# Block-sparse attention on gathered keys: tiles of two query blocks with the twelve key blocks that they see

## The chip, the cores and the metric

The kernel runs on one core of one Trainium2 chip. The metric is the device time of one execution in microseconds. Three executions of the kernel before took 979.37, 981.89 and 981.99 us, so its time is the median, 981.89 us. The profile is of one more execution, whose span is 978.8 us.

The engines have short names here: PE multiplies matrices (PEld is its weight load), DVE, ACT and POOL work on vectors, and SP issues most transfers to the DMA engines. PE writes its products to PSUM, whose banks hold 512 fp32 numbers per partition.

## The reference

```python
# q, k, v: (4 batches, 8 heads, 768 tokens, 64); blocks of 32 tokens, 24 of them
mask = np.abs(blk_i - blk_j) <= 1
mask = mask | (blk_i == 0) | (blk_j == 0) | (blk_i == 23) | (blk_j == 23)
for qb in range(24):
    for kb in sampled_blocks[qb]:            # three, drawn at random
        mask[qb*32:(qb+1)*32, kb*32:(kb+1)*32] = True
scores = np.where(mask, q @ k.T / 8, -1e9)
attn = softmax(scores)                       # denominator + 1e-9
x = (attn @ v)                               # to (3072 tokens, 512)
h = x @ w_in                                 # 512 -> 2048, weights in float64
out = np.maximum(0.01 * h, h) @ w_out        # 2048 -> 512
```

So a query block in the middle sees its own and the two neighbouring blocks, the first and the last block, and three sampled ones; the first and the last query block see all 24. A sampled block may be one that is seen anyway, or be drawn twice; it counts once.

## The kernel before

All products run on fp16 pairs: an fp32 number is scaled by a power of two and split into a high and a low part. A feed-forward product takes three products of parts, scores take two products whose 128 rows stack high and low parts, and the product with V takes two.

**Attention is dense.** The work is cut into 12 items (batch b, run j of 256 tokens) of 16 units; a unit is 128 queries of one head against all 768 keys. Per unit: PE writes scores of 128x768 to PSUM (`unit_scores`, four products, L541, one buffer of two banks); DVE scales them, adds the mask and takes the row's extreme (L551, `unit_ttr`); ACT takes the exponential and its sum (L556); DVE works out the reciprocal (L561, L562); ACT writes the high part of the weights (L571) and DVE the low part (L577), except for the first 32 units, for which ACT scales (L567) and POOL writes both parts (L568, L575). One transposing transfer on SP turns the pair into `pt`, twelve blocks of 128x128 (L582). Two units share the product with V: twelve products of 256 columns (L592). ACT and DVE evacuate it (L604, L607), and split it into x (L615, L617).

**Masks** for all 768 keys are built once as `masks`, of bf16, by POOL (L241). V and K are prepared per batch: scaled, split and, for K, transposed by SP (L484, `kt`); V stays in SBUF in fp16 parts. Q is prepared per half of a run and transposed twice (L511, L514).

**Feed-forward** runs in chunks of 128 hidden units, 16 an item: 12 products of 256 columns (L631), ACT and DVE take the leaky maximum (L639, L645), ACT writes the high part (L652) and POOL the low part (L655), and 6 products of 512 columns (L664) add to two output banks, which are scaled (L681, L684) and sent out (L687).

**Weights** arrive as the bits of float64. Per 128x512 ACT squares the upper word (L274), DVE shifts and joins (L279, L282, L284) and zeroes tiny values (L287). PE sums the squares for the scale (L201), and ACT and POOL or DVE split.

**The order.** The program is unrolled; every engine runs its instructions in program order. One step per unit issues a piece of each kind of work by a string of letters ("tdocqmxgsvbaph" here: reduction, reciprocal, output product, and so on) and spreads preparations over the steps; from unit 32 on PE is held to the written order. Feed-forward chunks of an item come from 7 steps after its last unit. Weight preparation gets 3.2 pieces a step.

Of the kernel before, what the change touches and what calls it, by code (L numbers as in the profile page):

```python
# [25 lines left out]
TINY = 2.0 ** -60        # floor of a sum of squares  # L26
CFG = {                      # buffers, engines and order of the work
    "ahead": 2,
    "avl0": 3,
    "avlag": 3,  # L30
    "avt": 1,
    "bank": {'w': 'h', 'q': 'h', 'k': 'h', 'v': 'h'},
    "big": 1,
    "blog": 40,
    "bs": 1500,
    "bstep": 0,
    "ch": {'PE': 32},
    "cpos": 0,
    "early": 2,
    "fa": 2000,  # L40
    "flag": 2,
    "g": 4,
    "ghn": 1,
    "guard": 'v',
    "ht": 2,
    "k": 'adp',
    "keep": 1,
    "krate": 0.7,
    "kt": 4,
    "lead": 7,  # L50
    "lead0": 5,
    "mpos": 1,
    "ob": 4,
    "ord": 'tdocqmxgsvbaph',
    "p": 3,
    "pek": 0,
    "peq": 1,
    "pev": 0,
    "pew": 1,
    "pool": '1',  # L60
    "pooln": 2,
    "pp": 3,
    "ps_s": 1,
    "pt": 2,
    "q": 'add',
    "q0": 3,
    "qnb": 1,
    "qrate": 0.7,
    "qsb": 3,
    "quota": 1.6,  # L70
    "raw": 2,
    "rmax": 2,
    "rmin0": 0,
    "rqb": 3,
    "share": 0,
    "slag": 1,
    "spread": 12,
    "steady": 2,
    "tmp": 2,
    "tr": 0,  # L80
    "v": 'adp',
    "v0": 3,
    "v_at": 0,
    "vbufs": 6,
    "vl": 6,
    "vrate": 0.8,
    "w": ['app', 'app', 'app', 'app', 'app', 'app', 'adp', 'adp'],
    "wprio": 0,
    "wq": 'sync',
    "wr": [3.2, 3.2, 3.2, 3.2],  # L90
    "wrate": 3.2,
    "ws": None,
    "wt": 2,
    "xbufs": 3,
}
FLAG = 2                 # chunks of the hidden layer between its two products
GROUP = 2                # query tiles that share one product with V


# [3 lines left out]
def tile_block_sparse_attention_ffn(  # L103
# [13 lines left out]
):  # L117
    nc = tc.nc
# [4 lines left out]
    NJ = S // (2 * P)            # runs of 256 tokens  # L123
# [3 lines left out]
    HC = 2 * NC                  # (head of the pair, chunk)  # L127
    SCALE = 1.0 / float(np.sqrt(D))

# [4 lines left out]
    ps_s = ctx.enter_context(tc.tile_pool(name="ps_s", bufs=CFG["ps_s"], space=bass.MemoryType.PSUM))  # L134
    ps_o = ctx.enter_context(tc.tile_pool(name="ps_o", bufs=2, space=bass.MemoryType.PSUM))
    ps_1 = ctx.enter_context(tc.tile_pool(name="ps_1", bufs=1, space=bass.MemoryType.PSUM))

    def bank(name, tag="h"):
        if CFG["share"]:
            return ps_1.tile([P, 512], F32, tag="bank", name=name, bufs=CFG["share"])  # L140
        return ps_1.tile([P, 512], F32, tag=tag, name=name, bufs={"h": 3, "av": 1}[tag])

# [39 lines left out]
    def copy(out, in_, eng):  # L182
        if eng == "p":
            nc.gpsimd.tensor_scalar(out=out, in0=in_, scalar1=1.0, scalar2=1.0, op0=ALU.mult, op1=ALU.mult)
        elif eng == "a":
            nc.scalar.activation(out, in_, AF.Copy)
        else:
            nc.vector.tensor_copy(out=out, in_=in_)

    eye = cst.tile([P, P], BF16, name="eye")  # L190

    def squares(parts, name, fl):
        """Sum of the squares of fp32 tiles [P, k * 128], cut to bf16, as the trace
        of products on the tensor engine: [P, 1], to be summed over the partitions."""
        now = tc.cur_priority
        tc.cur_priority = now - CFG["bs"]
        pb = bank(f"{name}_sq", CFG["bank"][fl])
        blocks = [t.bitcast(BF16).rearrange("p (n l) -> p n l", l=2)[:, c:c + P, 1]
                  for t in parts for c in range(0, t.shape[1], P)]
        for i, t in enumerate(blocks):  # L200
            nc.tensor.matmul(pb[:, :P], t, t, start=(i == 0), stop=(i == len(blocks) - 1))  # L201
        ss = sm.tile([P, 1], F32, tag=f"ss{fl}", name=f"{name}_ss")
        junk = sm.tile([P, P], F16, tag="tr", name=f"{name}_tr", bufs=1) if CFG["tr"] else pb[:, :P]
        nc.vector.tensor_tensor_reduce(
            out=junk, in0=pb[:, :P], in1=eye, scale=1.0, scalar=0.0, op0=ALU.mult, op1=ALU.add, accum_out=ss)
# [4 lines left out]
    masks = cst.tile([P, NJ, S], BF16, name="masks")  # L210

    allow = cst.tile([NB, NB], F32, name="allow")
    iota = cst.tile([NB, NB], F32, name="iota")
    hot = cst.tile([NB, NJ, P], F32, name="hot")
    sb = cst.tile([NB, 2 * NR], I32, name="sb")
    sf = cst.tile([NB, NR], F32, name="sf")

    def load_constants():
        nc.sync.dma_start(out=eye, in_=c_eye)
        nc.sync.dma_start(out=allow, in_=c_allow)  # L220
        nc.sync.dma_start(out=iota, in_=c_iota)
        nc.sync.dma_start(out=hot, in_=c_hot)
        nc.sync.dma_start(out=sb, in_=sampled.bitcast(I32))

    def build_masks():
        nc.vector.tensor_copy(out=sf, in_=sb.rearrange("p (a b) -> p a b", b=2)[:, :, 0])
        eq = cst.tile([NB, NB], F32, name="eq")
        for r in range(NR):
            nc.vector.tensor_scalar(out=eq, in0=iota, scalar1=sf[:, r:r + 1], scalar2=None, op0=ALU.is_equal)
            nc.vector.tensor_tensor(out=allow, in0=allow, in1=eq, op=ALU.max)  # L230
        pm = bank("mask_ps")
        for j in range(NJ):
            nc.tensor.matmul(pm[:, j * NB:(j + 1) * NB], hot[:, j, :], allow, start=True, stop=True)
        m24 = cst.tile([P, NJ * NB], F32, name="m24")
        nc.vector.tensor_scalar(out=m24, in0=pm[:, :NJ * NB], scalar1=-1.0, scalar2=-NEG, op0=ALU.add, op1=ALU.mult)
        for j in range(NJ):
            mj = masks[:, j, :].rearrange("p (a i b) -> p a i b", a=NJ, i=2)
            src = m24[:, j * NB:(j + 1) * NB].rearrange("p (a b) -> p a b", a=NJ)
            src = src.unsqueeze(3).to_broadcast([P, NJ, NB // NJ, BLOCK // 2])
            for i in range(2):  # L240
                nc.gpsimd.tensor_scalar(  # L241
                    out=mj[:, :, i, :].rearrange("p a (b c) -> p a b c", c=BLOCK // 2), in0=src,
                    scalar1=1.0, scalar2=1.0, op0=ALU.mult, op1=ALU.mult,
                )

    pf = ctx.enter_context(tc.tile_pool(name="pf", bufs=2))
# [6 lines left out]
    W = pw.tile([P, 2 * NQ, NP, WI], F32, name="W")  # L253
    W16 = W.rearrange("p a b c -> p (a b c)").bitcast(F16).rearrange("p (a b l c) -> p a b l c", a=2 * NQ, b=NP, l=2)
# [816 lines left out]
```

## Time and profile before

| | |
|---|---|
| Times of three executions | 979.37, 981.89, 981.99 us |
| Profiled execution, span | 978.8 us, 16568 instructions |
| ACT busy, of the span | 696.0 us (71%) |
| Transfers | 137.48 MB, 140 GB/s mean |
| Transposes on SP | 192 `pt`, 24 + 24 Q, 16 K |
| Other transfers on SP | 117 |

The profile counts an engine as busy while an instruction runs; several at once on PE overlap, and their ends are modelled. "Mean ns" is the duration of one instruction, and an engine's start-to-start distance can be a little less. The idle time that stands behind a group is that of the engine just before it, with the instruction that ended most of it. The rows of the stages, of the chain and of SP's issues are quoted where the prediction uses them.

### The profile page before, as it was taken

What the parts mean: (1) busy time and instruction counts of PE and PEld (TensorE: products, weight loads), DVE (VectorE), ACT (ScalarE), POOL (GpSimd) and SP (SyncE); (2) the same over time, 40 slices, a digit from 0 to 9 for tenths busy, and PEclk for the clock granted to TensorE, in tenths of its full rate; (3) what the DMA queues carried; (4) which work ended last, traced back from release to release, by engine and by line L of the source; (5) the groups of instructions that cost most, each with busy time, mean ns of one, the idle gap of its engine ahead of it and who ended that gap; (6) DMA issues with size and microseconds to landing.
All of it is one profiled execution on the core that took longest, in us unless ns stands there. A gap on an engine that the chain in (4) does not pass through costs nothing. (4 is left out here: it accounts for less than half of the span.)

```text
span 978.8 us, 16568 instructions
## 1 busy us (share of the span) xinstructions
PE 825.8 (84%) x5638; PEld 560.5 (57%) x5638; DVE 772.3 (79%) x1837; ACT 696.0 (71%) x1357; POOL 324.1 (33%) x342
## 2 busy tenths in 40 slices
PE   2534636675889899999898899998999999999998
PEld 1212324443556566666675566766666766767665
DVE  4999899989977987888687678887787888777311
ACT  2856666565778887788786878887787877777433
POOL 3477566776411321232221121232221111212222
PEclk9995666888999999999999999999999999999999
DMA  9977766758599686666898777678687766756100
GB/s 244 237 154 182 154 161 160 146 119 172 99 199 198 120 168 129 130 130 119 181 198 166 141 134 131 119 130 161 132 151 139 137 124 127 127 92 130 33 22 22
DMA packets 423028, 137.48 MB, mean 140 GB/s; under 512 B 378888, under 2 KB 415776, under 8 KB 422944
## 3 DMA queue, kind: packets, MB, share of 16 engines
q1 hardware_dynamic: 422944, 136.43, 69.7%
q8 instruction: 44, 0.72, 0.3%
q14 instruction: 40, 0.33, 0.1%
HBM read 35.73 MB, written 6.29 MB: 43 GB/s over the span
## 5 line engine op out<-in xcount | busy, mean ns | idle before, releaser
L655 POOL TENSOR_TENSOR g<-ht,g 128x256 f16<-128x256 f32 x192 | 149.6, 780 | 481.3 <-ACT g L652 431.7
L664 PE MATMUL o<-W,g 128*128 128x512 f16 x1152 | 282.0, 381 | 6.1 <-POOL g L654 1.8
L631 PE MATMUL h<-x,W 128*128 128x256 f16 x2304 | 286.0, 274 | 0.0
L631 PEld LDWEIGHTS <-W 128*128 128x128 f16 x2304 | 227.5, 100 | 46.8
L556 ACT ACTIVATE p<-p,mx 128x768 f32<-128x768 f32 x192 | 178.8, 931 | 93.5 <-DVE mx L551 84.6
L551 DVE CUSTOM_DVE_ANT_0 p<-s,masks,nsc 128x768 f32<-128x768 f32 x192 | 193.9, 1010 | 16.4 <-PE s L541 14.4
L577 DVE SCALAR_TENSOR_TENSOR pp<-p,r,pp 128x768 f16<-128x768 f32 x160 | 166.9, 1044 | 48.9 <-ACT pp L571 47.5
L664 PEld LDWEIGHTS <-g 128*128 128x128 f16 x1152 | 112.2, 98 | 124.3 <-issue 5.5
L541 PE MATMUL s<-kt_k,qs_q 128*128 128x512 f16 (+1 forms) x384 | 100.5, 345 | 74.4 <-DVE mx L551 66.5
L592 PE MATMUL av<-pt,v 128*128 128x256 f16 x1152 | 152.6, 285 | 12.1 <-DVE xf L607 7.1
L571 ACT ACTIVATE pp<-p,r 128x768 f16<-128x768 f32 x160 | 148.3, 928 | 16.2 <-DMA pt<-pp 9.2
L592 PEld LDWEIGHTS <-v 128*128 128x128 f16 x1152 | 117.3, 102 | 48.8 <-issue 11.2
L645 DVE SCALAR_TENSOR_TENSOR ht<-h,gd,ht 128x256 f32<-128x256 f32 x160 | 76.5, 479 | 49.4 <-ACT ht L639 48.6
L541 PE MATMUL s<-kt_k,qxs_q 128*128 128x512 f16 (+1 forms) x384 | 101.2, 348 | 0.4 <-DMA qxs_q<-qn_q 0.4
L639 ACT ACTIVATE ht<-h,gs 128x256 f32<-128x256 f32 x160 | 73.7, 460 | 31.3 <-PE h L631 29.8
L652 ACT ACTIVATE g<-ht 128x256 f16<-128x256 f32 x176 | 71.8, 408 | 28.0 <-DVE ht L645 26.8
L541 PEld LDWEIGHTS <-qs_q 128*128 128x128 f16 x384 | 38.2, 101 | 91.5 <-issue 73.9
L561 DVE TENSOR_SCALAR den<-sum 128x1 f32<-128x1 f32 x192 | 28.3, 147 | 47.1 <-ACT p L556 46.8
L575 POOL TENSOR_TENSOR pp<-p,pp 128x768 f16<-128x768 f32 x32 | 59.1, 1850 | 1.5
L541 PEld LDWEIGHTS <-qxs_q 128*128 128x128 f16 x384 | 39.5, 103 | 30.1 <-issue 5.6
L607 DVE SCALAR_TENSOR_TENSOR xf<-av,avt 64x256 f32<-64x256 f32 x96 | 41.0, 427 | 14.0 <-ACT avt L604 11.3
L568 POOL TENSOR_SCALAR pp<-p 128x768 f16<-128x768 f32 x32 | 32.6, 1018 | 51.6 <-ACT p L567 51.6
(115 smaller groups left out, 824.3 us busy)
## 6 DMA issues: line engine op xcount, KB each, us to landing
raw_wi<-in_moe_w_in_dram SPq DMA_DIRECT2D x16, 512.0 KB, 4.2
raw_wo<-in_moe_w_out_dram SPq DMA_DIRECT2D x16, 512.0 KB, 4.0
rk<-in_k_dram SPq DMA_DIRECT2D x16, 384.0 KB, 4.3
rq<-in_q_dram SPq DMA_DIRECT2D x24, 256.0 KB, 3.6
v<-in_v_dram SPq DMA_DIRECT2D x16, 384.0 KB, 4.4
out_dram<-ob SPq DMA_DIRECT2D x24, 256.0 KB, 2.0
pt<-pp SPq DMA_TRANSPOSE x192, 4.0
qs_q<-rq SPq DMA_TRANSPOSE x24, 3.2
```

The source lines that it names most:

```text
L541: nc.tensor.matmul(sp[:, c0 * P:c1 * P], st[:, col, :], kt[:, u.hh * NC + c0:u.hh * NC + c1, :].rearrange("p c t -> p (c t)"), start=(n == ...
L551: nc.vector.tensor_tensor_reduce(out=u.p, in0=u.sp, in1=masks[:, u.j, :], scale=u.nsc, scalar=3.0e38, op0=ALU.add, op1=ALU.min, accum_out= ...
L556: nc.scalar.activation(u.p, u.p, AF.Exp, scale=-1.0, bias=u.nm_, accum_out=u.sum)
L571: nc.scalar.activation(u.pp[:, 0, :], u.p, AF.Copy, scale=u.r)
L577: nc.vector.scalar_tensor_tensor(out=u.pp[:, 1, :], in0=u.p, scalar=u.r, in1=u.pp[:, 0, :], op0=ALU.mult, op1=ALU.subtract)
L592: nc.tensor.matmul(g.av[:, :n], vt[:, g.hh, c, :], g.pt[:, l * NC + c, :n], start=(c == 0 and l == 0), stop=(c == NC - 1 and l == 1))
L631: nc.tensor.matmul(c.ph[:, :N2], W16[:, 2 * b, d, wl, o:o + P], it.x[:, xl, d, :N2], start=(d == 0 and m == 0), stop=(d == NP - 1 and m == 2))
L639: nc.scalar.activation(t, c.ph[:, :n], AF.Copy, scale=scale[1])
L645: nc.vector.scalar_tensor_tensor(out=t, in0=c.ph[:, :n], scalar=scale[0], in1=t, op0=ALU.mult, op1=ALU.max)
L652: nc.scalar.activation(g[:, 0, :], t, AF.Copy)
L655: nc.gpsimd.tensor_tensor(out=g[:, 1, :], in0=t, in1=g[:, 0, :], op=ALU.subtract)
L664: nc.tensor.matmul(it.po[t], c.g[:, gl, t * P:(t + 1) * P], W16[:, 2 * (c.f // PER) + 1, c.f % PER, wl, :], start=(c.first and m == 0), st ...
```

## The change

Attention no longer runs over all keys. A tile T is 64 queries, two neighbouring query blocks (2T-1 and 2T), with twelve key blocks: four around the two, the first and last block, and six sampled ones, 384 keys. T = 0 holds query blocks 0 and 23 and keeps all 768 keys, in two parts of 384. A unit is a tile and a *pair* of heads: scores of the two heads stand on partitions 0 to 63 and 64 to 127 of one bank. There are again 192 units (12 tiles x 4 batches x 4 head pairs), with 208 parts.

- **K**: for each tile DVE copies the four neighbouring blocks and the two outer ones of all heads from `kt` (L493, L494), and POOL copies six sampled blocks, each behind a load of its index into a register (L499, L500). The mask per slot is spread to 384 columns by POOL (L505).
- **V**: the prepared parts of a batch are written to a buffer in DRAM, and nine transfers on SP bring a tile's twelve blocks back (L515, L518, L523), six of them behind an index load on SP (L521). There are two buffers `vg`.
- **Units**: scores are four products of 64 partitions x 384 columns (L548), one step ahead, with two buffers of one bank. The reduction (L557), exponential (L568), high (L584, ACT) and low part (L591, DVE, for every unit) have 128x384. A transposing transfer has six blocks (L594). The product with V is 12 products of 128x128 for two units (L606), 24 at T = 0. Evacuation takes two instructions on ACT and DVE for two units (L617, L621), two on POOL (L625, L632) and one on ACT (L630).
- **Feed-forward**: a chunk has two blocks of 128 hidden units, so that its vector instructions have 512 columns (L654, L658, L664); the high part moves from ACT to DVE (L663). The products are the same.
- **Weights**: ACT's square becomes an absolute value (L267), a maximum with a small number on DVE (L268) takes the place of the last guard, and a step gets 4 pieces.
- **Order**: "dstSocmxgvabphw"; PE is held to the written order from step 16.

```diff
+    def gather_k(b, T):
+        nc.vector.tensor_copy(out=kg[:, :, :P], in_=kt[:, :, t0:t0 + P])
...
+        for slot, i in sampled_of(T):
+            off = nc.gpsimd.value_load(offs[:1, i:i + 1], min_val=0, max_val=S - BLOCK)
+            nc.gpsimd.tensor_copy(
+                out=kg[:, :, slot * BLOCK:(slot + 1) * BLOCK], in_=kt[:, :, bass.ds(off, BLOCK)])
...
+    def gather_v(b, T):
+        nc.sync.dma_start(out=vg[:, 0, :], in_=scr[b][t0:t0 + P, :])
...
+        for slot, i in sampled_of(T):
+            off = nc.sync.value_load(offs[:1, i:i + 1], min_val=0, max_val=S - BLOCK)
+            nc.sync.dma_start(out=vg[ps, c, :], in_=scr[b][bass.ds(off, BLOCK), :])
...
     def unit_scores(u):
-        sp = ps_s.tile([P, 1024], F32, tag="s", name=f"s_{u.nm}")[:, :S]
-        for n, st in enumerate((qs, qxs)):
-            for c0, c1 in ((0, 4), (4, NC)):
-                nc.tensor.matmul(
-                    sp[:, c0 * P:c1 * P], st[:, col, :],
...
+            sp = ps_s.tile([P, 512], F32, tag="s", name=f"s_{u.nm}_{part}")[:, :KEYS]
+            for n, st in enumerate((qs, qxs)):
+                for hh in range(2):
+                    nc.tensor.matmul(
+                        sp[hh * D:(hh + 1) * D, :], st[:, h, c0:c0 + Q2], keys,
+                        start=(n == 0), stop=(n == 1))
...
-                nc.tensor.matmul(
-                    g.av[:, :n], vt[:, g.hh, c, :], g.pt[:, l * NC + c, :n],
+                    nc.tensor.matmul(
+                        pr.av[:, u.pi, hh], vt, u.pt[c // NCH][:, :, c % NCH, hh * D:(hh + 1) * D],
...
+            nc.vector.tensor_scalar(out=big, in0=big, scalar1=1.125 * 2.0 ** -15, scalar2=None, op0=ALU.max)
-            if g != "m":
-                (nc.gpsimd if g == "p" else nc.vector).scalar_tensor_tensor(
-                    out=dst, in0=big, scalar=2.0 ** -30, in1=dst, op0=ALU.is_ge, op1=ALU.mult)
```

How the instructions stand on two engines shows best in their order. On SP before, in the second half of the prepared Q of a middle item, the queue holds transposes of softmax weights (`pt<-pp`), two of Q and a load of Q:

```order
L582 DMA_TRANSPOSE pt_2_1_4736<-pp_2_1_1_4728 128x12x128
L511 DMA_TRANSPOSE qs_q_2_1_4931<-rq_2_1_4469 128x8x128
L582 DMA_TRANSPOSE pt_3_0_4861<-pp_3_0_0_4791 128x12x128
L514 DMA_TRANSPOSE qxs_q_2_1_4934<-qn_q_2_1_4689 128x8x128
L451 DMA rq_1_0_5930<-in_q_dram 128x4x128
L582 DMA_TRANSPOSE pt_3_0_4861<-pp_3_0_1_4853 128x12x128
```

On SP after, in the second batch, the gather of V for one tile stands behind two transposes (`scr` is the buffer in DRAM, `offs` the indices, ISA the register instructions of a load and of an address):

```order
L594 DMA_TRANSPOSE pt_1_1_0_0_10527<-pp_1_1_0_0_10524 128x6x128
L594 DMA_TRANSPOSE pt_1_1_1_0_10576<-pp_1_1_1_0_10573 128x6x128
L515 DMA vg_6_10618<-scr_8509 128x1024
L518 DMA vg_6_10618<-scr_8509 32x1024 x2
L521 TENSOR_LOAD offs
L521 ISA x2
L523 ISA
L523 DMA vg_6_10618<-scr_8509 32x1024
```

The last four rows come five times more before the next transpose: where two transposes of softmax weights followed each other, nine transfers and six index loads now stand between them once per tile.

On PE before, the score products of one unit (`s`, from the stacked keys `kt` and the two forms of Q) write 128 partitions, by 512 and 256 columns:

```order
L541 LDWEIGHTS qs_q_1_1_4063
L541 MATMUL s_2_0_0_4473<-kt_k_2_3109,qs_q_1_1_4063 128x512
L541 LDWEIGHTS qs_q_1_1_4063
L541 MATMUL s_2_0_0_4473<-kt_k_2_3109,qs_q_1_1_4063 128x256
```

On PE after, in the first batch, the scores of a unit are followed by a second feed-forward product and that by the products with V:

```order
L548 LDWEIGHTS qs_q_0_1_4898
L548 MATMUL s_0_2_2_0_5119<-kg_2_4685,qs_q_0_1_4898 64x384
...
L548 LDWEIGHTS qxs_q_0_1_4901
L548 MATMUL s_0_2_2_0_5119<-kg_2_4685,qxs_q_0_1_4901 64x384
...
L674 LDWEIGHTS g_1_8_4755
L674 MATMUL o_1_8_0_5124<-W,g_1_8_4755 128x512
...
L674 MATMUL o_1_8_1_5131<-W,g_1_8_4755 128x512
...
L606 LDWEIGHTS vg_1_5003
L606 MATMUL av_0_1_0_5141<-pt_0_1_0_0_4816,vg_1_5003 128x128
...
L606 MATMUL av_0_1_0_5141<-pt_0_1_1_0_4876,vg_1_5003 128x128
```

Rows that repeat are left out: each score product stands there twice in turn, for the one head and the other, each form of `o` six times and each form of `av` six times. Score products have moved from two column counts on all partitions to half the partitions, and the weights of a product with V now serve 128 columns instead of 256.

More of the change, by code (lines that the diff above doesn't have):

```diff
@@ L231, in build_masks @@
[L231 to L244, printed above, removed]
@@ new lines, in require_kg, with require_v, side_step @@
+    def require_kg(b, T):
+        for hp in range(NP):
+            until(("k", b, hp), lambda: (b, hp) in kready)
+        until(("kg", b, T), lambda: (b, T) in kgs)
+    def require_v(b, hp, T):
+        until(("v", b), lambda: (b, hp) in v16s if T == 0 else (b, "ready") in scr)
+        while T and (b, T) not in vgs:
+            start_gather_v()
+    quota = [0.0]
+    def side_step(amount):
+        quota[0] = min(quota[0] + amount, 2 * amount)
+        while flows and quota[0] > 0:
+            c = next(flows[0], "end")
@@ new lines, in tile_block_sparse_attention_ffn, with hs_step, av_step @@
+    step = 0
+    units = [u for it in items for u in it.units]
+    def hs_step(both=True):
+        if pend_hs:
+            pu = pend_hs.popleft()
+            unit_high(pu)
+            unit_split(pu)
+            if pu.pi == 1:
+                pend_av.append((step + (CFG["av_lag0"] if step < 16 else CFG["av_lag"]), pu.pair))
+    def av_step():
+        if pend_av and pend_av[0][0] <= step:
+            pr = pend_av.popleft()[1]
+            pair_av(pr)
+            vfree[0] += pr.hp == NP - 2 and pr.T > 0
+            evs.append(pair_evac(pr))
```

1097 lines of the change are left out of this document (522 added, 575 removed).

## The prediction, made before the changed kernel was run

> **What bounds the kernel now.** I read three views: the busy times of the page, the busy times by stretches of time, and the chain of work that ended last. First the page's totals and four stretches; the columns of a stretch are its length, then busy time (and instructions) of PE, weight loads, DVE, ACT and POOL, the granted clock, the DMA share and GB/s.
>
> ```profile
> PE 825.8 (84%) x5638; PEld 560.5 (57%) x5638; DVE 772.3 (79%) x1837; ACT 696.0 (71%) x1357; POOL 324.1 (33%) x342
> ...
> 75.00:100.00 25.00, 11.71 (x54) 6.58 (x54) 24.68 (x38) 15.67 (x27) 16.75 (x13) 0.57 0.73 170
> ...
> 150.00:175.00 25.00, 14.20 (x87) 9.49 (x86) 24.76 (x44) 15.63 (x28) 19.02 (x14) 0.70 0.79 182
> ...
> 300.00:400.00 100.00, 94.78 (x671) 65.05 (x669) 85.42 (x216) 81.63 (x167) 24.76 (x30) 1.00 0.77 149
> ...
> 925.00:979.00 54.00, 49.88 (x334) 32.42 (x332) 9.17 (x20) 18.81 (x41) 12.03 (x18) 1.00 0.05 20
> ```
>
> No engine is full over the whole span, but in each stage one is. Up to about 245 us DVE is busy 24.7 of 25 us: it decodes the weights. From there PE is busy 95%, and the last 54 us are feed-forward alone. The chain shows how fast PE goes when nothing holds it:
>
> ```profile
> 885.62 0.65 PE s L541 x4
> 886.27 1.29 PE o L664 x6
> 887.57 1.31 PE h L631 x12
> ...
> 890.82 1.31 PE av L592 x12
> ```
>
> So scores cost 0.65 us for 4 products (1536 columns), both feed-forward products 2.60 for one chunk of 128 hidden units, and 12 products with V 1.31. Over the program: feed-forward 192 x 2.60 = 499 us, V 96 x 1.31 = 126, scores 192 x 0.65 = 125; together 750 of 979. A check of the method: of this, 34 of the 192 units of scores (22 us) and about 15% of V (19 us) lie before 245; the other 709 at 95.5% (between the 94.78 above and the higher later stretches) are 742, and 245 + 742 + 4 us of last output is 991. That is 12 too many, since a few feed-forward chunks run before 245. The working is made against the profiled span, 978.8 us; the single times lie 0.6 to 3.2 us above it, so 2 us are added at the end.
>
> **The part up to the last weights.** The square sum of the last weights (first row, of the weights' tile) shows where this stage ends; the other rows are groups of DVE, with busy time, mean ns and idle time before them.
>
> ```profile
> L204 DVE CUSTOM_DVE_ANT_0 wo_sq<-wo_sq,eye x4: 279/286/300, 62.1 to 236.6; 128x128 f32<-128x128 f32 x4
> ...
> L551 DVE CUSTOM_DVE_ANT_0 p<-s,masks,nsc 128x768 f32<-128x768 f32 x192 | 193.9, 1010 | 16.4 <-PE s L541 14.4
> L577 DVE SCALAR_TENSOR_TENSOR pp<-p,r,pp 128x768 f16<-128x768 f32 x160 | 166.9, 1044 | 48.9 <-ACT pp L571 47.5
> L645 DVE SCALAR_TENSOR_TENSOR ht<-h,gd,ht 128x256 f32<-128x256 f32 x160 | 76.5, 479 | 49.4 <-ACT ht L639 48.6
> L607 DVE SCALAR_TENSOR_TENSOR xf<-av,avt 64x256 f32<-64x256 f32 x96 | 41.0, 427 | 14.0 <-ACT avt L604 11.3
> L287 DVE SCALAR_TENSOR_TENSOR W<-big_wi,W 128x512 f32<-128x512 f32 x16 | 19.6, 1222 | 0.0
> L188 DVE COPY rq<-qn_q 128x512 f16<-128x512 f16 x24 | 11.4, 475 | 0.0
> L287 DVE SCALAR_TENSOR_TENSOR W<-big_wo,W 128x512 f32<-128x512 f32 x16 | 17.0, 1060 | 0.0
> L279 DVE TENSOR_SCALAR W<-raw_wo 128x512 int32<-128x512 int32 x16 | 11.0, 685 | 0.1
> ```
>
> DVE's own sum hardly moves. The guard L287 goes (36.6 us); a maximum on 128x512 takes its place, by L279 32 x 0.69 = 22, so -15. A score reduction of 384 columns lies between 479 ns at 256 and 1010 at 768, about 0.61: 36 of them instead of 34 x 1.01 are -12. The split of the softmax weights is on DVE from the start: 34 x 0.62 = +21. K's gather has two DVE copies of 1024 and 512 columns, by L188 0.95 + 0.48: for 7 tiles +10. Evacuation is 34 x 0.43 against about 12: +3. Net +7. Against that, two POOL passes of the early units are gone, beside which DVE was stretched (the last row gives least, median and most):
>
> ```profile
> L575 POOL TENSOR_TENSOR pp<-p,pp 128x768 f16<-128x768 f32 x32 | 59.1, 1850 | 1.5
> L568 POOL TENSOR_SCALAR pp<-p 128x768 f16<-128x768 f32 x32 | 32.6, 1018 | 51.6 <-ACT p L567 51.6
> ...
> L284 DVE SCALAR_TENSOR_TENSOR W<-raw_wo,W 128x512 int32<-128x512 int32 x16 | 17.9, 1119 | 0.0
> ...
> L284 DVE SCALAR_TENSOR_TENSOR W<-raw_wo,W x16: 664/898/2124, 36.1 to 230.2; 128x512 int32<-128x512 int32 x16
> ```
>
> L284's fastest instance is 0.66, its mean 1.12. If a stretch of 0.4 us went on each of the 96 remaining large decode operations (32 each of L282, L284 and the shift L279), that would be -38; if none went, 0. I take half, -19, so the stage ends at 245 + 7 - 19, about 232; bounds 214 and 252.
>
> **The products on PE.** The score products now have 384 columns and write 64 partitions; a part has four of them, two heads by turns. By the chain's 0.65 us for 1536 columns a part costs 0.65 if they go one by one, and 0.33 if the two halves of the partitions run beside each other. No row of before has a product that writes 64 partitions; the ends are a factor of two apart, and I take 0.45. The products with V have 128 columns, each with its own weight load. The nearest rows, of weight loads, of the weights' square sums, and of the timeline:
>
> ```profile
> L631 PEld LDWEIGHTS <-W 128*128 128x128 f16 x2304 | 227.5, 100 | 46.8
> ...
> L201 PE MATMUL wo_sq<-W x64: 217/286/312, 44.8 to 236.0; 128*128 128x128 bf16 x64
> ...
> 44.83 1.01 PE L201 MATMUL wo_sq<-W 128*128 128x128 bf16 x8
> ```
>
> Eight such products take 1.01 us, the last one 0.286 of it, so (1.01 - 0.286)/7 = 0.103 each: the loads, 0.10, then set the pace, not the columns (1.31/12/2 = 0.055). I take 0.103, with 0.055 as lower bound. So a product with V of half the width is no cheaper, and there are 1248 of them instead of 1152. After 232 us: feed-forward 495 (some 5 before), V 0.85 x 1248 x 0.103 = 109 (58 to 109), scores (208 - 36) x 0.45 = 77 (57 to 112). That is 681; at 95.5% 713, and the span is 232 + 713 + 4 = **949**. The PE ends of both give 232 + 610/0.955 + 4 = 875 and 232 + 716/0.955 + 4 = 986.
>
> The row bears on a rule of the Trainium skill, page "TensorE: Matmul & The Clock Gate", Part 3, "Packing small matmuls — row/col tiling": products whose outputs lie on other partition groups run at the same time, three of them 2.38 times as fast. By it, as an estimate with the same 79% yield for two, a part costs 0.41 and the span is 942; no run here shows it yet.
>
> **DVE, ACT and POOL after that.** Call a tile of 64 queries with all eight heads T: 48 of them, four units each, and two double chunks of feed-forward. DVE per T: 4 x (0.61 + 0.62 + 0.43), 2 x (0.74 by the row below for the maximum and about 0.55 for the high part), 1.4 gather, 0.6 norms, 1.3 for Q and K: 12.5 us. PE's 713 us over 40 T and 83 us of backlog are near 15.5, so DVE stays covered. ACT loses the high part of the hidden layer and half of exp and high part, and falls. POOL: two low parts by 1.43, six copies by 0.57, the additions of evacuation 2.1, the mask about 0.8: 9.2 plus six loads of an index.
>
> ```profile
> L684 DVE SCALAR_TENSOR_TENSOR ob<-o,beta,ob 128x512 f32<-128x512 f32 x12 | 8.7, 743 | 0.7 <-PE o L664 0.6
> L363 POOL TENSOR_TENSOR W<-W 128x512 f16<-128x512 f32 x24 | 33.8, 1429 | 2.9 <-ACT W L362 2.9
> L654 POOL TENSOR_SCALAR g<-ht 128x256 f16<-128x256 f32 x16 | 9.0, 566 | 22.2 <-DVE ht L645 11.4 <-DVE r L562 7.7 <-PE wo_sq L201 1.9
> ```
>
> **SP's queue, the new place.** SP issues each transfer in program order, and the next one waits behind it. Issue times (least, median, most), two rows of the timeline, and the landing:
>
> ```profile
> L582 SPq DMA_TRANSPOSE pt<-pp x192: 1382/1485/3319, 35.5 to 907.7; - x192
> ...
> L511 SPq DMA_TRANSPOSE qs_q<-rq x24: 1232/1232/1932, 18.7 to 833.6; - x24
> ...
> L266 SPq DMA_DIRECT2D raw_wo<-in_moe_w_out_dram x16: 327/333/574, 27.6 to 220.4; - x16
> ...
> 502.90 1.27 SPq L514 DMA_TRANSPOSE qxs_q<-qn_q  x1
> 504.27 1.45 SPq L582 DMA_TRANSPOSE pt<-pp  x1
> ...
> out_dram<-ob SPq DMA_DIRECT2D x24, 256.0 KB, 2.0
> pt<-pp SPq DMA_TRANSPOSE x192, 4.0
> ```
>
> Twelve blocks take 1.48 us to issue and eight 1.23, so the new six about 1.16, plus the 0.1 gap between two issues: 4 x 1.26 = 5.0 per T. Nine gathers of V at 0.33 + 0.1: 3.9. Q, K, V and output: per T half a Q load with two transposes (1.6), a third of a K pair (0.8), V and output (0.6): 3.0. Together 11.9 us per T where before had about 8. To it come six index loads from SBUF into a register (L521), each with three register instructions. No row of before has one: not under the gap of 0.1, since the next issue needs the register, and not over a whole small transfer to memory and back, 2.0. The nearest row in kind is one issue, 0.33; with its register instructions and gaps I take 0.6: 15.5 per T. For 37 tiles with gather, 5% of waits, 3 first tiles at 14 and 65 us of feed-forward after the last tile (10 double chunks of 5.2 stand behind the last product with V, and some of the work beside it): 232 + 37 x 16.3 + 42 + 65 = 942. So SP stands just under PE. Each 0.1 us of an index load is 23 us of span where SP binds. The gather waits for a V buffer (two of them), which the products with V two tiles earlier set free; behind it on SP stand the transposes of the next softmax weights, and for their landing, 4 us later, wait PE's next products with V; behind POOL's six loads stands the low part of the hidden layer, for which PE's second product waits.
>
> **Rivals.**
> *A, forecast*: PE keeps the bound, SP under it or level: 949, from 915 to 970. For: the sums above, and that PE is the only engine above 90% in the middle. Against: two queues within 1% of each other seldom overlap wholly. Chance 0.45.
> *B, PE lighter*: scores beside each other, V's loads partly hidden as all loads of before are, and index loads of 0.4 us: PE alone down to 875, SP 232 + 37 x 14.3 x 1.05 + 107 = 895; so 870 to 915. Against: the 0.103 of the nearest row. Chance 0.15.
> *C, no gain*: an index load costs two issues with their gap, 2 x 0.33 + 0.1 = 0.76. SP needs 16.5 per T: 232 + 37 x 17.3 + 107 = 979. Chance of ending within the bound around it 0.08. The Trainium skill, page "DMA: Bandwidth & Descriptors", "Latency and other measured facts", gives a floor of about 600 ns for a `tensor_load`; with 0.15 of checks, an estimate, that is this case, 976. No row here shows one.
> *D, slower*: the same queue with index loads of 1.0 us or more, half of the 2.0 of the landing row: 17.9 per T, 232 + 37 x 18.8 + 107 = 1035; at 2.0 it is 1268. It decides from 0.78 on. The same end comes without SP if scores go one by one and V stays at 0.103: 986. For it: nine more issues per T in a queue that runs in order. Against: SP was issuing only about 408 us (192 x 1.48, 64 x 1.3, 117 x 0.35) of 979. Chance 0.30.
> *E, the gather spares DVE nothing*, because an operation of 384 columns costs nearer 0.75 than 0.61: then DVE has 13.6 per T, still under 15.5, and the time is A's plus some 5 for the first stage, 955. Chance 0.02.
>
> **How the numbers follow.** The time is A's, 949 + 2 = **951**. The range takes in A, most of B, C and D up to an index load of 1.05 us: **880 to 1045**. A measurement tells about 0.3% from no change. A, B and E make faster 0.62; C the same, 0.08; D slower, 0.30.
>
> **What would show it.** Right: DVE full up to 225 to 240 us, then PE above 93% in the middle stretches, the new scores under 0.5 us a part in the chain, products with V near 1.24 us for 12, SP's index loads under 0.7 us. Wrong: PE under 85% in the middle with SP's issues back to back, transposes that wait behind the gather, and the chain going through pt's landing; or, for B, 12 products with V in 0.7 us.

## The result, and the profile after

The changed kernel takes 1061.66 us (1059.78 to 1063.15), against 981.1 us before in the same rounds: a ratio of 1.083, with a 95% interval of 1.081 to 1.085. It is 8% slower. The span of the profiled execution grew from 978.8 to 1058.7 us.

First the page's busy times and the stretches of the kernel after, with the columns as in the prediction:

```profile
PE 775.7 (73%) x5772; PEld 489.1 (46%) x5772; DVE 712.3 (67%) x1963; ACT 569.4 (54%) x1289; POOL 384.5 (36%) x625
...
300.00:400.00 100.00, 73.42 (x576) 47.80 (x574) 69.06 (x198) 53.50 (x125) 36.42 (x62) 0.90 0.70 148
...
500.00:600.00 100.00, 73.66 (x574) 46.39 (x573) 62.01 (x178) 51.76 (x122) 31.41 (x54) 0.86 0.64 135
...
1000.00:1058.70 58.70, 54.82 (x362) 35.14 (x359) 11.78 (x20) 9.80 (x15) 11.99 (x11) 1.00 0.05 19
```

Every engine has less to do than before, POOL apart, and none is full in the middle. PE, which was at 93 to 95% there, is at 73 to 74% in these two stretches. The chain shows what PE costs where it is not held (of the kernel after):

```profile
905.64 2.62 PE h L647 x24
908.26 0.45 PE s L548 x4
908.70 0.78 PE av L606 x12
```

A part's scores cost the 0.45 us that were taken, and twelve products with V 0.78 where 1.24 were. So PE has *less* work than forecast. What holds it stands in the waits of PE (total us, times and longest over the whole run; those of the weights' stage are left out), first before, then after:

```profile
PE s L541 <- DVE mx L551: 66.5, 49, 3.6
```

```profile
PE s L548 <- DMA qs_q<-qa_q: 46.4, 6, 14.4
...
PE q_sum L127 <- ACT qn_q L442: 33.5, 7, 8.6
PE av L606 <- DMA pt<-pp: 28.2, 12, 5.0
```

Before there is one steady short wait, for the score buffer: behind 240 us it makes up 29 of 33 us. After, PE stands for Q's transposes up to 14 us at a time, for the square sum of Q that it needs first, and for the transposes of the softmax weights. All three need transfers that SP issues; Q also needs its preparation on ACT and DVE in time. The three longest waits for Q's transposes, 14.0, 14.4 and 12.3 us, end at 356, 586 and 809 us, once at each change of batch. The longest, from 571 us, on PE's timeline (start, duration, what, idle time before it):

```profile
571.67 0.38 PE L127 MATMUL q_sum<-ss_q,ones 128*128 128x1 f32 x2
586.42 0.53 PE L548 MATMUL s<-kg,qs_q 128*64 128x384 f16 x2 [14.37 <-DMA qs_q<-qa_q]
587.67 0.53 PE L548 MATMUL s<-kg,qxs_q 128*64 128x384 f16 x2 [0.71 <-DMA qxs_q<-qn_q]
588.13 4.48 PE L674 MATMUL o<-W,g 128*128 128x512 f16 x12
```

Twelve output products take 4.48 us after this gap and 2.76 elsewhere; the granted clock is 0.50 from 575 to 590 us and 1.00 from 595. This gap cost more than its length.

The same sums for several kernels, from the last weights to PE's last product. "Busy" is the time in which a product runs and "idle" the rest, both by the trace; two columns give the idle time that Q and the transposes of the softmax weights ended. "At the chain's rates" is an estimate of what the same products would take unhindered: their counts times the chain's rows, with 1.29 us for six output products in every kernel. E1, e6, e9 and e14 are experiments below.

| us | from | busy | at the chain's rates | idle | for Q | for softmax weights | time |
|---|---|---|---|---|---|---|---|
| before | 240 | 701 | 684 | 34 | 0 | 0 | 981 |
| after | 225 | 694 | 641 | 136 | 78 | 17 | 1062 |
| fixed places (e1) | 225 | 679 | 637 | 88 | 41 | 2 | 1002 |
| early Q (e6) | 225 | 692 | 637 | 115 | 4 | 44 | 1039 |
| fixed places, early Q (e9) | 225 | 676 | 634 | 66 | 1 | 3 | 973 |
| fixed places, merged, early Q (e14) | 225 | 689 | 641 | 83 | 11 | 1 | 1000 |

From before to after: 15 us gained up to the last weights and 43 on PE's work at the chain's rates, 36 lost because products ran slower than that (53 us above the rates instead of 17, at a mean granted clock of 0.93 instead of 1.00), and 102 lost in idle time. That gives the 80 us of the result.

SP's index loads and gathers (of the kernel after; least, median, most in ns), and one gather on its timeline:

```profile
L521 SPq TENSOR_LOAD <-offs x264: 262/273/978, 30.4 to 969.9; - x132
L521 SPq FUSED_REGOPS  x264: 152/155/187, 30.9 to 970.2; - x132
...
L594 SPq DMA_TRANSPOSE pt<-pp x208: 1210/1239/2582, 36.7 to 978.7; - x104
```

```profile
610.80 0.47 SPq L515 DMA_DIRECT2D vg<-scr  x1
611.32 0.89 SPq L518 DMA_DIRECT2D vg<-scr  x2
612.41 5.65 SPq L523 DMA_DIRECT2D vg<-scr  x6
618.17 1.28 SPq L454 DMA_TRANSPOSE qs_q<-qa_q  x1
```

Six transfers with their loads take 5.65 us, 0.94 each, and the whole gather is a block of over 7 us, behind which the transposes stand. From 400 to 800 us SP's instructions, waits left out, add up to 328 us, 82%, and 95 parts pass, 21.9 tiles:

```profile
400.00:600.00 200.00, 24.40 (x184) 27.91 (x46) 0.88 0.65 137
600.00:800.00 200.00, 24.51 (x196) 29.80 (x49) 0.96 0.67 140
```

(PE and DVE on the score tiles alone; DVE's counts are the parts.) So SP issues 15.0 us per tile, and a tile takes 18.3: neither SP nor PE is full. The two V buffers, for which the prediction let the gather wait, hold SP for only 9 us behind 225 us.

What the block does to the transposes can be read from the ends and starts of rows, behind 240 us: from the end of the DVE instruction that finishes a pair of softmax weights to the issue of its transpose it took 4.5 us on average in the kernel after, 2.8 before, and 2.3 in e1 below, which has no index loads.

### The profile page after: what moved, and what is told of

Read it like the earlier page. It is cut to its first block, busy times and chain, and to the rows that moved or that the text cites. A ratio compares the mean times of both kernels' runs of the same rounds, so it can differ in the third digit from the quotient of the medians.

```text
span 1058.7 us, 20177 instructions
## 1 busy us (share of the span) xinstructions
PE 775.7 (73%) x5772; PEld 489.1 (46%) x5772; DVE 712.3 (67%) x1963; ACT 569.4 (54%) x1289; POOL 384.5 (36%) x625
## 5 line engine op out<-in xcount | busy, mean ns | idle before, releaser
L591 DVE SCALAR_TENSOR_TENSOR pp<-p,r,pp 128x384 f16<-128x384 f32 x208 | 137.7, 675 | 89.2 <-ACT pp L584 84.1
L664 POOL TENSOR_TENSOR g<-ht,g 128x512 f16<-128x512 f32 x96 | 112.9, 1176 | 207.5 <-DVE g L663 184.7
L584 ACT ACTIVATE pp<-p,r 128x384 f16<-128x384 f32 x208 | 121.6, 608 | 108.2 <-DMA pt<-pp 68.1
L568 ACT ACTIVATE p<-p,mx 128x384 f32<-128x384 f32 x208 | 126.7, 609 | 92.2 <-DVE mx L557 71.5
L557 DVE CUSTOM_DVE_ANT_0 p<-s,em,nsc 128x384 f32<-128x384 f32 x176 | 107.8, 614 | 71.0 <-PE s L548 69.0
L500 POOL COPY kg<-kt 128x256 f16 x264 | 119.0, 469 | 84.8 <-PE s L548 49.9
L606 PE MATMUL av<-pt,vg 128*128 128x128 f16 x1056 | 83.4, 231 | 49.0 <-DMA pt<-pp 28.2
L625 POOL TENSOR_TENSOR xf<-avt 128x128 f32<-128x128 f32 x96 | 49.4, 515 | 185.7 <-DVE avt L621 185.6
L548 PE MATMUL s<-kg,qs_q 128*64 128x384 f16 x352 | 67.2, 379 | 53.1 <-DMA qs_q<-qa_q 46.1
L606 PEld LDWEIGHTS <-vg 128*128 128x128 f16 x1056 | 68.6, 103 | 76.6 <-issue 55.7
L617 ACT ACTIVATE avt<-av 64x256 f32<-64x256 f32 x192 | 72.7, 379 | 46.5 <-PE av L606 43.8
L632 POOL TENSOR_TENSOR x<-xf,x 128x128 f16<-128x128 f32 x96 | 50.8, 529 | 128.0 <-ACT x L630 127.8
L654 ACT ACTIVATE ht<-h,gs 128x512 f32<-128x512 f32 x80 | 54.3, 679 | 72.5 <-PE h L647 72.3
L621 DVE SCALAR_TENSOR_TENSOR avt<-av,avt 64x256 f32<-64x256 f32 x192 | 80.5, 419 | 17.3 <-ACT avt L617 12.2
L658 DVE SCALAR_TENSOR_TENSOR ht<-h,gd,ht 128x512 f32<-128x512 f32 x80 | 59.6, 745 | 40.8 <-ACT ht L654 40.8
L548 PEld LDWEIGHTS <-qs_q 128*64 128x64 f16 x416 | 25.4, 113 | 125.8 <-DMA qs_q<-qa_q 47.5
L548 PE MATMUL s<-kg,qxs_q 128*64 128x384 f16 x352 | 63.7, 360 | 3.7 <-DMA qxs_q<-qn_q 3.7
L663 DVE CAST g<-ht 128x512 f16<-128x512 f32 x96 | 42.9, 447 | 23.9 <-PE o L674 23.3
```

The costliest lines, as they stand in the source:

```text
L500: nc.gpsimd.tensor_copy(out=kg[:, :, slot * BLOCK:(slot + 1) * BLOCK], in_=kt[:, :, bass.ds(off, BLOCK)])
L548: nc.tensor.matmul(sp[hh * D:(hh + 1) * D, :], st[:, h, c0:c0 + Q2], keys, start=(n == 0), stop=(n == 1))
L557: nc.vector.tensor_tensor_reduce(out=u.p[i], in0=u.sp[i], in1=kgs[u.b, u.T][1] if u.T else zero.to_broadcast([P, KEYS]), scale=u.nsc, scal ...
L568: nc.scalar.activation(u.p[i], u.p[i], AF.Exp, scale=-1.0, bias=u.mx[:, :1], accum_out=u.pair.sum[:, u.pi, i:i + 1])
L584: nc.scalar.activation(pp[:, 0, :], p, AF.Copy, scale=u.r)
L591: nc.vector.scalar_tensor_tensor(out=pp[:, 1, :], in0=p, scalar=u.r, in1=pp[:, 0, :], op0=ALU.mult, op1=ALU.subtract)
```

## The experiments

Times are medians; ratios are to the kernel before, with 95% intervals. Eighteen kernels ran. Three theories stood first: the rate of SP's queue (1), Q's late loading and preparation (2), POOL's gather of K (3).

**e1, fixed places.** 1001.8 us, ratio 1.021 [1.009, 1.033].

```diff
-            off = nc.sync.value_load(offs[:1, i:i + 1], min_val=0, max_val=S - BLOCK)
-            nc.sync.dma_start(out=vg[ps, c, :], in_=scr[b][bass.ds(off, BLOCK), :])
+            off = (i * 7) % NB * BLOCK
+            nc.sync.dma_start(out=vg[ps, c, :], in_=scr[b][off:off + BLOCK, :])
```

> The six sampled key blocks of V are fetched from fixed places, without the six index loads per tile on SP; the nine transfers per tile stay. The gathered V is not that of the sampled blocks. Theory 1, SP's issue rate sets the pace (18.8 us per tile from 232 to 985 us): six loads of some 0.5 us go, 3 us per tile on 44 tiles, so up to 130 us less, 930 to 960 us, where PE takes over. Theory 2, the late loads of Q set the pace (PE waits 46 us for Q's transposes and 33 us for its square sums): less than 30 us, above 1030. Theory 3, POOL's gather of K: no change.

The run takes away the loads and the addresses from registers together. The 60 us are half of what theory 1 wanted, and twice what theory 2 allowed. PE's waits of e1 show where they come from; with the loads gone, Q's square sum and the softmax weights are almost always there in time:

```profile
PE s L547 <- DMA qs_q<-qa_q: 34.5, 4, 12.1
...
PE q_sum L127 <- ACT qn_q L442: 4.9, 3, 2.4
...
PE av L605 <- DMA pt<-pp: 2.3, 5, 0.7
```

**e2, V in two transfers.** 994.4, ratio 1.013 [1.006, 1.021].

```diff
-        for slot, a in ((4, 0), (5, S - BLOCK)):
...
+        nc.sync.dma_start(out=vg[:, 1:, :], in_=scr[b][:2 * P].rearrange("(c p) x -> p c x", p=P))
```

> V's gather is two transfers per tile, of 128 and 256 fixed rows, without index loads: the bytes stay, eight issues become one. The gathered V is not that of the sampled blocks. Theory 1: SP has about 6 us less per tile on 44, more than PE leaves room for, so the time is PE's own, 900 to 930 us. Theory 2: above 1020. Theory 3: no change.

Seven transfers fewer per tile bring 7 us beyond e1, whose two executions lie 8 us apart. Theory 1 in its plain form falls: SP has room now, 232 us of instructions from 400 to 800 us, and PE still waited 48.5 us for Q's transposes.

**e3, Q loaded early**: 1046.7, ratio 1.067 [1.058, 1.075]. **e4, K from fixed places**: 1069.9, ratio 1.090 [1.083, 1.098].

```diff
-        if step % 8 == 1:
-            get_q(step // 8 + 1)
+        if step % 8 == 5:
+            get_q(step // 8 + 2)
```

The loaded Q blocks get a second buffer for it and the outputs one less.

> Q's load is issued five steps earlier into a second buffer (one output buffer is given up for the space). Theory 1: SP has the same work, so within 15 us of 1062. Theory 2: the 33 us of PE waiting for Q's square sums go, and part of the 46 us for its transposes: 990 to 1030. Theory 3: no change.

> POOL copies six key blocks of K from fixed places, without the six index loads per tile on POOL. The gathered K is not that of the sampled blocks. Theory 1 and 2: within 15 us of 1062. Theory 3, scores come late because POOL's gather is slow: more than 40 us less, under 1020.

Theory 3 is out. E3 gained 15 us, at the edge of what theory 1 allowed and short of theory 2. In e3 the wait for the square sum is gone from PE's waits, but 44 us for Q's transposes remain: Q's preparation, not only its load, is late. Preparations wait in one line, and at a change of batch V's and K's stand ahead of Q's.

**e5, one load of six indices**: 1036.2, ratio 1.057 [1.049, 1.064]. **e6, Q loaded early and prepared first**: 1039.1, ratio 1.059 [1.052, 1.067]. **e7, both**: 1024.7, ratio 1.045 [1.038, 1.052].

```diff
+        _, all_off = nc.values_load_multi_w_load_instructions(
+            offs[:1, i0:i0 + 2 * NR], engines=[mybir.EngineType.SP], min_val=0, max_val=S - BLOCK)
...
-        flows.append(gen)
+        (flows.appendleft if key[0] == "q" else flows.append)(gen)
```

> The six indices of a tile come with one load instruction into six registers, ahead of the transfers; the six transfers use them. Same computation, all nine transfers. Theory 1 (SP's issue rate): five of six loads' fixed cost goes, about 0.3 us each, and the rest no longer stands in one block of 5.6 us: 1010 to 1035, between the 1062 of the change and the 1002 without loads. Theory 2 (late preparation of Q): 1050 to 1062.

> Q's load five steps earlier into a second buffer, and Q's preparation ahead of K's and V's in the queue of preparations. Theory 2a, Q is late because it stands behind the preparation of V and K (PE waits 46 us for Q's transposes): 1000 to 1020. Theory 1: SP still holds the pace, 1035 to 1050, like the earlier load alone (1047).

> Both: one index load per tile, and Q's load and preparation early. Theory 1 with 2a as the second cause: 945 to 980, at least 25 us under the better of the two alone, since each uncovers the other. If either theory is wrong, no better than the better one alone.

One load of six values took 1.29 us (median), against 6 x 0.27, so it saves little by itself; e5 still gained 26 us. There the load stands ahead of the block, at the median 24 us before the first of the six transfers, so that the nine issues of a gather take 4.6 us (median) instead of 7.3, as long as without loads (4.5 in e1). In e6 PE's waits for Q fall from 84 to 9 us, and PE waits in another place (its waits, of e6):

```profile
PE av L606 <- DMA pt<-pp: 51.3, 29, 6.6
...
PE s L548 <- DMA qs_q<-qa_q: 5.8, 2, 5.0
```

The transposes of the softmax weights now hold PE 51 us instead of 28, and the gathered V 25 instead of 5: most of what Q no longer takes is waited for elsewhere. e7 was 11 us under the better of the two, not 25, and far above the 945 to 980 expected: with the load moved out of the block, the two gains of 26 and 23 us do not add up.

**e8, feed-forward earlier** (e7 with a spread of 6): 1042.4, ratio 1.063 [1.052, 1.073].

> As the one before, and feed-forward chunks are issued at twice the rate for the same backlog (a spread of 6 steps instead of 12). The attention ends with 14 to 17 double chunks left, 74 to 89 us of PE alone, in the runs so far. If PE's idle time in the attention stage can take five of them: 15 to 26 us less than the run before. If PE has no idle time there that is not already behind a wait in its own order: within 8 us of it.

A miss on both branches: 18 us *slower* than e7. More feed-forward in PE's written order did not fill the gaps: behind 225 us PE idles 109 us instead of 98.

**e9, fixed places and early Q**: 972.6, ratio 0.991 [0.988, 0.993].

> The six sampled blocks of V from fixed places without index loads (the gathered V is not that of the sampled blocks), and Q's load and preparation early. Without loads alone 1002, with early Q alone 1039, against 1062. Theory: SP's loads and Q's late preparation are two causes in a row, the one hiding the other; then 945 to 975, some 30 to 50 us under the run without loads, as PE waited 35 us there for Q's transposes. Rival: those waits are a place where another shortage shows (the transposes' buffers, POOL, the order): within 15 us of 1002.

The time is as the theory said. PE's waits of e9:

```profile
PE av L605 <- DMA pt<-pp: 6.0, 5, 2.5
PE s L547 <- DMA qs_q<-qa_q: 5.8, 1, 5.8
```

With both changes the waits for Q and for the transposes are 12 us together instead of 108. The two changes bring 89 us together, about the sum of the 60 and 23 that each brings alone. That one cause hides the other is not shown by these times: the 6 us between 83 and 89 are within the 8 us that lie between the two executions of e1.

**e10, indirect gathers on POOL, early Q**, the whole computation: 993.2, ratio 1.011 [1.000, 1.022].

```diff
+        for c in range(2):
+            nc.gpsimd.indirect_dma_start(
+                out=vg[:, 1 + c, :], out_offset=None, in_=scr[b][:, :],
+                in_offset=bass.IndirectOffsetOnAxis(ap=vidx[:, c, T - 1:T], axis=0))
```

> The whole computation. Eight of the nine transfers of V per tile become two indirect gathers of 128 rows on POOL, with row numbers worked out once; SP keeps one transfer and has no index load; Q is loaded and prepared early. If SP's queue and Q are the causes: 940 to 980, under the kernel before. If POOL, whose queue now builds the descriptors, becomes the next bound, or the gathers' descriptors hold DVE up: 990 to 1040.

```profile
L535 POOL DMA_INDIRECT vg<-scr,vidx x88: 942/986/1637, 86.4 to 902.0; - x88
```

POOL pays 1 us per gather (of e10: least, median, most), SP is relieved, and 68 us come back, 46 of them beyond e6 with its early Q; it ends on the second branch.

**e11, indices kept in registers, early Q, outer blocks in one transfer**: 1017.1, ratio 1.036 [1.031, 1.041]. **e12, V prepared 12 steps earlier as well**: 1019.4, ratio 1.039 [1.034, 1.044].

```diff
+        if T not in kept:
+            _, kept[T] = nc.values_load_multi_w_load_instructions(...)
+        all_off = kept[T] if T <= 7 else kept.pop(T)
...
+        nc.sync.dma_start(
+            out=vg[:Q2, 1, :], in_=scr[b].rearrange("(n l) x -> n l x", l=BLOCK)[0:NB:NB - 1])
```

> The whole computation. The indices of tiles 1 to 7 are loaded once into registers and kept for all batches, those of tiles 8 to 11 with one load per tile and batch, without range checks: 23 loads instead of 264, and the two outer blocks of V come in one transfer. Q is loaded and prepared early. If index loads and Q are the causes: like the run with fixed blocks and early Q, 960 to 985, a few us to either side of the kernel before. If fixed places made the transfers themselves cheaper (a fixed address costs no register work): 990 to 1015.

> As the one before, and V of the next batch is loaded and prepared 12 steps earlier (from batch 2 on), away from the change of batch. The gaps of PE left in the run with fixed blocks and early Q (77 us after 225, against 38 in the kernel before) lie mostly at the changes of batch. If V's preparation there is what holds the engines: 10 to 20 us less than the run before. If it is the dense first tile itself (twice the vector work in four steps) or K's preparation: within 5 us of it.

A surprise: with a tenth of the loads, e11 is 44 us above e9. V's preparation at the change of batch is not what holds the rest. The next two runs take the differences to e9 apart.

**e13, e11 without the merged transfer**: 993.6, ratio 1.013 [1.010, 1.016]. **e14, e9 with the merged transfer**: 999.7, ratio 1.020 [1.014, 1.026].

> As the run with kept indices and early Q, but the two outer blocks of V come in two transfers again, so that SP's order is that of the run with fixed places and early Q but for the loads and register addresses. If the merged transfer made that run slow: 970 to 985. If transfers with an address from a register (and the 23 loads left) cost it: 1005 to 1025.

> As the run with fixed places and early Q, with the two outer blocks of V in one transfer: no index loads, no register addresses, the merged transfer. The gathered V is not that of the sampled blocks. If the merged transfer is what costs: 1005 to 1025. If registers are: 965 to 980.

| early Q in all four | outer blocks apart | merged |
|---|---|---|
| fixed places | 973 (e9) | 1000 (e14) |
| registers, 23 loads | 994 (e13) | 1017 (e11) |

Merging costs 23 to 27 us, registers with 23 loads 17 to 21, within the noise independent of each other. That one issue *less* per tile costs 25 us was in no theory. In e14 ACT waits 48.2 us for Q's transposes to free their buffer and 47.2 for those of the softmax weights, 21.5 and 17.2 in e9. One thing in SP's own waits goes with the merged transfer: SP stands for the landing of gathered V before a transpose of softmax weights, 19.5 us in e14 and 6.1 in e11, never in e9 and e13. That is less than the 25 us, and why the landing is waited for stays open. Of the 20 us for registers, the loads and the addresses were not told apart.

**e15, e10 with a fourth buffer of split weights**: 995.9, ratio 1.016 [1.011, 1.020]. **e16, indices of tiles 1 to 7 kept, indirect gathers for 8 to 11, early Q**: 1000.6, ratio 1.023 [1.018, 1.027]. **e17, e16 with the fourth buffer**: 990.9, ratio 1.012 [1.009, 1.016].

> The whole computation, as the run with indirect gathers and early Q, with four buffers for the split softmax weights instead of three (two output buffers for the space). ACT waited 29 us there for a transpose to free one. If that wait holds the rest: 970 to 985. If it is slack: within 8 us of 993.

> The whole computation. Indices of tiles 1 to 7 are loaded once (seven loads in all) and kept in registers; tiles 8 to 11 take eight of their blocks of V by two indirect gathers on POOL; Q is loaded and prepared early. Against 994 with 23 loads: if the sixteen loads of 1.3 us left in the stages after the first, in front of transposes, are the rest of the 20 us to the run with fixed places: 970 to 985. If register-addressed transfers themselves are: 988 to 1000.

> As the one before with four buffers for the split softmax weights (two output buffers). With indirect gathers alone the fourth buffer took 24 us of ACT's wait away and left the time as it was. If SP's full queue makes that wait cost here, where six transfers per tile remain: 10 us or more less than the run before; else within 6 us.

In e15 ACT's wait for those buffers fell from 29 to 5 us and the time stayed: slack. In e17 the same buffer gained 10 us, where SP issues more. E16, with 7 loads, is no faster than e13 with 23, so the sixteen loads alone are not the rest; its gathers on POOL differ too. No version with the whole computation came below the kernel before; e10, e17 and e13 are nearest, 1.1 to 1.3% above it and not told apart.

**e18, the kernel before with 288 index loads on SP**: 1011.5, ratio 1.034 [1.029, 1.038].

```diff
+        count[0] += 1
+        if count[0] % 4 == 0:
+            for i in range(6):
+                nc.sync.value_load(offs[:1, i:i + 1], min_val=0, max_val=S - BLOCK)
```

> The kernel before, with six index loads on SP behind the transpose of every fourth unit, 288 in all, whose values are not used. If it is the full queue that makes loads cost: SP was issuing 565 us of 979 there, so 288 x 0.55 = 158 us more fit into its waits, and the time stays within 1% (975 to 990). If a load on SP costs by itself, by the delay of the transposes behind it: 1000 to 1040, like the 60 us that 264 of them cost in the changed kernel.

This run decides whether the queue must be full for loads to cost. The 565 us of the expectation are too many: SP's instructions in the kernel before add up to 495 of 979 us. With the loads it is 665 of 1009 us, 155 of them the loads with their arithmetic and checks. The queue has room, and still 32 us are lost, 0.11 per load. A wait of PE, whose row in the kernel before had 66.5 us, and two of ACT in e18; the second had 3.1 us before and the third 9.2:

```profile
PE s L545 <- DVE mx L555: 84.7, 49, 7.4
```

```profile
ACT qn_q L497 <- DMA qxs_q<-qn_q: 27.8, 14, 3.3
...
ACT pp L575 <- DMA pt<-pp: 2.6, 5, 1.2
```

So here the queue need not be full for a load in it to cost. The delay shows at Q's transposes, for which ACT now waits 28 us, and only weakly at those of the softmax weights, which are issued 3.3 us after their pair is finished instead of 2.8. How it gets from there to PE's wait for the score buffer, through ACT and DVE that each run in order, is argued and not shown.

## Why the prediction was wrong, step by step

- **Up to the last weights: right in time, not in what fills it.** Forecast 232 us against 245; the square sum of the last weights came at 220.3 instead of 236.6, 16 us earlier against 13 forecast. DVE's decode operations did get shorter (L284 1.07 us, its successor L275 0.79), but DVE, forecast full, is busy 21.7 and 17.9 of 25 us in two stretches of the kernel after, where it had 24.7 and 24.8 before:

```profile
L173 DVE CUSTOM_DVE_ANT_0 wo_sq<-wo_sq,eye x4: 293/300/300, 68.2 to 220.3; 128x128 f32<-128x128 f32 x4
```

```profile
75.00:100.00 25.00, 10.82 (x76) 6.42 (x76) 21.74 (x51) 17.26 (x38) 11.51 (x17) 0.93 0.90 205
150.00:175.00 25.00, 9.72 (x65) 6.25 (x62) 17.94 (x47) 11.89 (x25) 6.74 (x6) 0.50 0.66 185
```

- **Scores on PE: right.** 0.45 us per part, the value taken: the two halves of the partitions run beside each other for the most part. The Trainium skill's rule in "TensorE: Matmul & The Clock Gate", Part 3, on packing agrees with this trace; the estimate worked out from it was 0.41.
- **Products with V: too dear.** Taken at 0.103 us from the square sums of the weights; measured 0.78/12 = 0.065, near the lower bound of 0.055. The weight load, 0.10 us long, is mostly hidden with 128 columns too. With this term PE's work after 232 us would have been 641 instead of 681.
- **An index load on SP: right in price.** Taken at 0.6 us with its register work; 0.27 + 0.155 + 0.018 measured for load, arithmetic and check, with gaps some 0.5 to 0.6. The floor of 600 ns in the Trainium skill's "DMA: Bandwidth & Descriptors", "Latency and other measured facts", does not hold for these loads from SBUF: the least was 262 ns.
- **SP's sum: right.** 15.5 us per tile forecast with the gaps between issues, 15.0 measured without them.
- **The step that failed: the span as the larger of PE's and SP's sums, with 4.5 to 5% of waits.** It allowed 32 us of waits behind the weights. PE idled 136 us there, and its products took 53 us above the chain's rates. Neither queue was full, SP at 82% and PE at 73% in the middle: what cost the time was that one's work was not ready when the other needed it, and the sum has no term for that. The gather's block of 7 us with the loads in it delays the transposes; ACT waits 68 us for the weights' buffers against 9 before and 25 in e1; PE waits 28 us for the landing and 84 for Q (46.4, 33.5, and 3.9 for its second transpose). E1, e6 and e9 show both parts: loads with register addresses and late Q take 60 and 23 us alone, 89 together.

```profile
L571 ACT ACTIVATE pp<-p,r 128x768 f16<-128x768 f32 x160 | 148.3, 928 | 16.2 <-DMA pt<-pp 9.2
```

```profile
L584 ACT ACTIVATE pp<-p,r 128x384 f16<-128x384 f32 x208 | 121.6, 608 | 108.2 <-DMA pt<-pp 68.1
```

- **Rival D named the right queue with the wrong mechanism.** It asked for loads of 1.0 us to make SP the bound at 1035. The loads were some half of that and SP was not full. Its counterargument, that SP was issuing only about 408 us before, took the transposes at their median; on average a `pt` transpose took 1.76 us, and the sum is 495. Q was not among the rivals at all: its preparation was counted as 3 us of SP per tile with K, V and the output, never as a step that must be done in time.
- **In the list of what would show it**, "PE under 85% in the middle" and "transposes that wait behind the gather" came true, though SP was not back to back. Of what was named for the forecast, scores under 0.5 us and loads under 0.7 us came true; DVE full in the first stage, PE above 93% and 12 products with V near 1.24 us did not. The 0.78 us for V is close to the sign of B.

E9 shows what is left: 225 us, 676 busy, 66 idle and 4 of last output are its span of 971. Even without late Q and without loads the changed kernel gains only 1% on the one before, since PE idles 66 us instead of 34 and its products take 42 us above the chain's rates instead of 17. The 66 us are spread over many short waits, and no run takes them apart.

## What to carry to other kernels

A sum per engine with a few per cent of waits was here a lower bound, not a forecast, although the fullest queue was at 82%. Price what is put into a queue by what stands behind it: in the kernel before, 288 loads on a queue that was issuing for half of the time cost 32 us. And when one late link is mended, look at the waits again before judging the mend: in e6 PE's waits for Q fell by 75 us and the time by 23.

## What was not expected of the hardware

After a gap of 14 us PE's granted clock was 0.50, and twelve products of 512 columns took 4.48 us instead of 2.76; some 5 us of work later the clock was back at 1.00:

```profile
575.00:580.00 5.00, 0.00 (x0) 0.00 (x0) 4.79 (x15) 2.62 (x7) 3.74 (x8) 0.50 0.52 102
...
585.00:590.00 5.00, 2.86 (x9) 0.99 (x10) 0.62 (x2) 0.71 (x2) 0.00 (x0) 0.50 0.51 105
590.00:595.00 5.00, 5.00 (x43) 3.00 (x41) 0.56 (x3) 0.76 (x2) 0.00 (x0) 0.84 0.36 85
595.00:600.00 5.00, 5.00 (x53) 4.12 (x51) 2.94 (x14) 3.48 (x9) 1.12 (x2) 1.00 0.81 157
```

One load of six indices takes 1.29 us, about as long as five single loads of 0.27: what loading together saves in the load itself is small, and what it gained in e5 goes with the load's place ahead of the block. And eight transfers per tile instead of nine, with the same bytes, were 23 to 27 us slower (e14 and e11), which no run here explains.
